# Threshold attention and an MLP mixer in one kernel: value groups two to a visit, one staging place for queries and keys, exponentials issued apart

## The chip, the cores and the metric

The kernel runs on one NeuronCore of a Trainium2 chip. The metric is the device time of one execution in microseconds (us). A profile is one execution recorded by the hardware profiler; its span runs from the first to the last instruction of the program. The engines are TensorE (PE in the profile, its weight loads PEld), VectorE (DVE), ScalarE (ACT), GpSimd (POOL) and SyncE (SP); DMAs are issued here from the queues of SP and ACT.

## What is computed

Eight batches, eight heads, 576 tokens, head size 64, all in float32. Attention keeps only scores that lie within tau of their row's maximum; its output, with the heads side by side (512 wide), goes through a token MLP and a channel MLP with residual sums.

```python
def _attn_ref(q, k, v, tau):
    scores = scale * np.matmul(q, k.transpose(0, 1, 3, 2))
    thresh = np.max(scores, axis=-1, keepdims=True) - tau
    scores = np.where(scores >= thresh, scores, -1000000000.0)
    scores = scores - np.max(scores, axis=-1, keepdims=True)
    attn = np.exp(scores)
    attn = attn / (np.sum(attn, axis=-1, keepdims=True) + 1e-09)
    return np.matmul(attn, v).astype(np.float32)

def _moe_ref(x, w_tok1, w_tok2, w_ch1, w_ch2):
    xt = x.transpose(0, 2, 1)
    h = np.maximum(xt @ w_tok1, 0.0) @ w_tok2
    u = x + h.transpose(0, 2, 1)
    h2 = np.maximum(u @ w_ch1, 0.0) @ w_ch2
    return (u + h2).astype(np.float32)
```

## The kernel before

**Units and visits.** Two heads make a pair, four pairs a batch (the code calls a batch a block, `b`). The work of two pairs is cut into nine units of 128 query rows: four of the first pair (t = 0 to 3), one that both pairs share for their last 64 rows (t = 4), four of the second (t = 5 to 8). The main loop (L529) visits the units in order, 144 of them in 16 windows of nine. The order of the instructions on every engine is the order in which this loop issues them; no scheduler changes it.

**One visit** of unit u issues, in this order:

- `scores(u)`: eight matmuls into two PSUM tiles (L301), a row maximum on VectorE for each head (L306), and a bias from it on GpSimd (L307).
- `norm(u - 1)`: reciprocals of the row sums on VectorE (L325, L326), a multiplication on GpSimd (L329).
- For unit u - 2 the transposition of its weights `e`. In block 0 TensorE does it (`turn`, L352), with copies on VectorE and ScalarE (L354). From block 1 on (`turn_blocks`) VectorE transposes 32 x 32 blocks into a tile T (L363), and when a group of two units is complete, 16 DMAs on SP's queue carry the blocks from T to their places in a tile eT (L373).
- `fill(0.4)`: mixer steps of an earlier block from a list, as many as a share of the visit's quota allows.
- `weigh(u)`: two Prelus (L316) read the scores out of PSUM into `e`, two Exps (L319) follow in place and give the row sums. All four are ScalarE's.
- `fill(0.6)`: more mixer steps.
- The loads for later pairs, the transposes of queries and keys of the next pair on VectorE (`prep`, L283) at t = 2 and t = 7, and last
- `values` (L385) for each group that is due: two matmuls of L403 and eight of L408 for a group of 256 query columns (each appears twice in the trace, since float32 goes through in two passes), and a copy from PSUM into xT on ScalarE (L413). A pair has two such groups, and a shared unit gives two of 64 columns. From block 1 on a group is due two visits after its DMAs were issued. That puts value groups into the visits with t = 1, 3, 5, 7 and (the two shared ones) 8.

**Mixer steps** are kept in the list `todo`: transposes of x (L425, copies L426 on ScalarE), the two matmuls of the token MLP (L434 with Relu L435 on ScalarE; L441 with an add L445 on VectorE), the first channel matmul (L463 with Relu L464 on ScalarE) and the second (L475, L479 with a copy L484 on VectorE and a store L485). The quota is the estimated cost of the list over the visits of a block. Until block 0 is through, there are none.

**Weights** come as 64-bit words in 31 pieces; `weight` turns them into float32 with small steps on ScalarE (L191, L193), VectorE (L201, L205, L209) and GpSimd (L215), and `load_piece` (L176) loads the next into one of four raw places from SP's queue. These steps run in the first 28 visits or so.

**Places.** PSUM: two tiles for scores (three in block 0), two `tr` tiles that transposes and value groups share, from block 1 on two `mm` tiles for the mixer. SBUF: staging tiles lq and lk for queries and keys in a pool with two places each; eT has two places, T two, `e` three.

**Loads of queries and keys.** A pair needs eight DMAs, four for each of lq and lk (L106). They are spread over visits t = 0 to 7, one part of lq and one of lk in each: on SP's queue in block 0 and on ScalarE's after. The loads for t = 0 to 3 belong to the pair whose `prep` is at t = 7, those of t = 4 to 7 to the one at t = 2 of the next window. Pair 1 is loaded at the start, before the values of pair 0 and the second weight piece (L242).

```python
        while due and due[0][0] <= u:
            _, b, p, c = due.popleft()
            values(b, p, c)
            if p == NP - 1 and c == 1:
                push(b)
```

Of the kernel before, what the change touches and what calls it, by code (L numbers as in the profile page):

```python
# [9 lines left out]
F32 = mybir.dt.float32  # L10
# [7 lines left out]
P = 128  # L18
# [3 lines left out]
def kernel(  # L22
# [26 lines left out]
    nc = tc.nc  # L49
    B, H, S, D = q.shape  # L50
# [14 lines left out]
    NK = 2 * S // P  # L65
# [4 lines left out]
    ld = ctx.enter_context(tc.tile_pool(name="ld", bufs=2))  # L70
    work = ctx.enter_context(tc.tile_pool(name="work", bufs=2))
# [11 lines left out]
    pairs = [(b, p) for b in range(B) for p in range(NP)]  # L83
# [9 lines left out]
    loaded = {}  # L93
    VL = 4
    vlast = [const.tile([P, P], F32, name=f"vl{i}") for i in range(VL)]

    def load_qk(n, eng, part=None):


        b, p = pairs[n]  # L100
        if n not in loaded:
            loaded[n] = [ld.tile([P, S // 32, 32], F32, tag=tag, name=f"{tag}_{n}") for tag in ("lq", "lk")]
        for i in range(4) if part is None else (part,):
            h, c = divmod(i, 2)
            for src, t, on in zip((q, k), loaded[n], eng):
                on.dma_start(  # L106
                    out=t[32 * i : 32 * i + 32], in_=src[b, 2 * p + h, :, 32 * c : 32 * c + 32].rearrange("(n t) d -> t n d", t=32)
                )

    def load_v(n):  # L110

        b, p = pairs[n]
        lv = ld.tile([P, NK, D], F32, tag="lv", bufs=4, name=f"lv_{n}")
        nc.sync.dma_start(out=lv, in_=v[b].rearrange("h s d -> (h s) d")[2 * S * p : 2 * S * p + 2 * S, :].rearrange("(c p) d -> p c d", p=P))
        vals[n] = lv
# [51 lines left out]
    def load_piece(i):  # L167
        if i >= len(pieces):
            return
        dst, src = pieces[i]  # L170
        rows = dst.shape[0]
        n = 1
        for d in dst.shape[1:]:
            n *= d
        raw = raw_at[i % NRAW][0:rows, 0 : n * (2 if wide(i) else 1)].bitcast(src.dtype)
        nc.sync.dma_start(out=like(raw, dst), in_=src)  # L176
        if wide(i):
            words = raw.bitcast(U32).rearrange("p (n w) -> p n w", w=2)
            h2 = work.tile([P, WMAX], F32, tag="o", name=f"h2_{i}")[0:rows, 0:n]
            raws[i] = like(words[:, :, 0], dst), like(words[:, :, 1], dst), like(h2, dst)  # L180
        else:
            raws[i] = like(raw, dst)
# [56 lines left out]
        weight(3 * i + 4 - steps_done)  # L239

    load_piece(0)
    load_qk(1, (nc.sync, nc.sync))  # L242
    load_v(0)
    for i in range(1, NRAW):
        load_piece(i)
# [24 lines left out]
    st = {}  # L270
    xTs = {}
    eTs = {}
    Ts = {}

    def in_blocks(b):
        return b > 0

    def prep(n):
        lq, lk = loaded.pop(n)
        made = []  # L280
        for src, name in ((lq, "qT"), (lk, "kT")):
            sb = work.tile([P, S], F32, tag=name, name=f"{name}_{n}")
            nc.vector.transpose(out=sb, in_=src.rearrange("p n d -> p (n d)"))  # L283
            made.append(sb)
        heads[n] = made
# [24 lines left out]
    def weigh(u):  # L310
        sc, bias = st.pop(u)
        rs = small.tile([P, 2], F32, tag="rs", name=f"rs_{u}")
        e = work.tile([P, 2 * S], F32, tag="e", bufs=3, name=f"e_{u}")
        for h in range(2):
            eh = e[:, S * h : S * h + S].rearrange("p (f x) -> p f x", f=2)
            nc.scalar.activation(out=eh, in_=sc[h][:, :, 0:HS], func=AF.Prelu, bias=bias[:, h : h + 1], scale=SCALE, alpha=STEEP)  # L316
        for h in range(2):
            eh = e[:, S * h : S * h + S]
            nc.scalar.activation(out=eh, in_=eh, func=AF.Exp, bias=ntau, accum_out=rs[:, h : h + 1])  # L319
        st[u] = e, rs  # L320

    def norm(u):
        e, rs = st[u]
# [8 lines left out]
    def group_of(u):  # L332

        b, p0, t = units[u]
        if t == SHARED:
            return (b, p0, "s"), 0, 1
        i, c = divmod(t - (t > SHARED), NI)
        return (b, p0 + i, c // 2), c % 2, 2

    def turn(u, third):  # L340

        key, place, n = group_of(u)
        e = st[u]
        if third == 0 and place == 0:
            eTs[key] = work.tile([P, NK * 2 * P], F32, tag="eT", name=f"eT_{u}")
        if third == 2:
            st.pop(u)
        eT = eTs[key][:, 0 : NK * n * P].rearrange("p (c x) -> p c x", c=NK)
        ps = ps_tr.tile([P, MAIN], F32, tag="tr", name=f"tr{third}_{u}")[:, 0 : 3 * P].rearrange("p (c x) -> p c x", c=3)
        for c in range(3):  # L350
            k0 = (3 * third + c) * P
            nc.tensor.transpose(out=ps[:, c, :], in_=e[:, k0 : k0 + P], identity=ident)  # L352
        on = nc.scalar.copy if third == 1 and u % 2 else nc.vector.tensor_copy
        on(out=eT[:, 3 * third : 3 * third + 3, P * place : P * place + P], in_=ps)  # L354

    def turn_blocks(u):

        key, place, n = group_of(u)
        e = st.pop(u)
        if place == 0:  # L360
            Ts[key] = work.tile([P, NK * 2 * P], F32, tag="T", name=f"T_{u}")
        T = Ts[key][:, 0 : NK * n * P]
        nc.vector.transpose(  # L363
            out=T.rearrange("p (a c n x) -> p c a n x", a=4, c=NK, n=n)[:, :, :, place, :],
            in_=e.rearrange("p (c a x) -> p c a x", c=NK, a=4),
        )
        if place == n - 1:
            del Ts[key]
            eTs[key] = work.tile([P, NK * 2 * P], F32, tag="eT", name=f"eT_{u}")
            w = NK * n * 32  # L370
            for a in range(4):
                for i in range(4):
                    nc.sync.dma_start(  # L373
                        out=eTs[key][32 * a : 32 * a + 32, w * i : w * i + w], in_=T[32 * i : 32 * i + 32, w * a : w * a + w]
                    )

    def split_middle(n):

        lv, vl = vals[n], vlast[n % VL]
        for h in range(2):  # L380
            r = slice(D * h, D * h + D)
            nc.gpsimd.tensor_copy(out=vl[r, r], in_=lv[r, NI, :])
        vals[n] = lv, vl
# [116 lines left out]
    def fill(share):  # L500
        nonlocal credit
        credit += share * quota
        while todo and credit > 0:
            cost, step = todo.popleft()
            credit -= cost
            step()
        if not todo:
            credit = 0.0
# [15 lines left out]

    prep(0)
    due = deque()
    b_now = 0
    LAG = 2
    for u in range(len(units) + LAG + 4):  # L529
        on = u < len(units)  # L530
        if u == UB:
            late.close()
            ps_mm = ctx.enter_context(tc.tile_pool(name="ps_mm", bufs=2, space=bass.MemoryType.PSUM))
        if on:
            b_now, p0, t = units[u]
            n = b_now * NP + p0
        w = u - LAG
        back = 0 <= w < len(units)
        if on:
            scores(u)  # L540
        if 0 < u <= len(units):
            norm(u - 1)
        if b_now:
            weight(2)
        if back:
            key, place, many = group_of(w)
            if in_blocks(key[0]):
                turn_blocks(w)
            else:
                for i in range(3):  # L550
                    turn(w, i)
            if place == many - 1:
                b, p, c = key
                if c == 0 and p % 2 == 0:
                    split_middle(b * NP + p)
                if c == "s":
                    split_middle(b * NP + p + 1)
                when = u + (2 if in_blocks(b) else 1)
                due += [(when, b, p + i, c) for i in range(2 if c == "s" else 1)]
        if b_now:  # L560
            fill(0.4)
        weight(2 if b_now else 1)
        if on:
            weigh(u)
        if b_now:
            fill(0.6)
        weight(2 if b_now else 1)
        if on:
            m = n + 2 + t // 4
            if t < 8 and m < len(pairs):  # L570
                load_qk(m, (nc.scalar if b_now else nc.sync,) * 2, t % 4)
                if t % 4 == 3:
                    load_v(m)
            if t == 2:
                prep(n + 1)
            if t == 7 and n + 2 < len(pairs):
                prep(n + 2)
# [5 lines that stand above are left out]
# [31 lines left out]
```

## Time and profile before

| | |
|---|---|
| times of five runs | 1395.74, 1398.53, 1400.26, 1400.70, 1401.69 us; median 1400.26 |
| profiled execution | 1400.26 us, its span 1398.5 us, mean granted TensorE clock 0.99 |
| busy: TensorE, VectorE, ScalarE, GpSimd | 1328.1, 587.6, 588.1, 357.5 us |
| costliest on TensorE | L479 389.1, L463 399.5, L301 190.2, L408 124.8, L441 77.0, L434 73.9 us |
| costliest on ScalarE | L319 220.1, L316 199.1, L464 85.9, L413 23.8 us |
| DMA | 128.34 MB, 92 GB/s on the mean |

A row of groups gives line, engine, operation, tiles and shape, then busy time and mean length; a row of the timeline gives start, length, engine, line, tiles and the number of instructions merged, and in brackets the idle time before the first of them with what ended it. A row of busy times by stretch gives for each of PE, PEld, DVE, ACT and POOL the busy time and the number of instructions, then the granted TensorE clock, the share of DMA engines that were busy, and GB/s. A busy TensorE is not one at its peak: at the change from one shape of matmul to another the next starts later, and the timeline counts that as busy; it shows only in the distance from start to start.

### The profile page before, as it was taken

What the parts mean: (1) busy time and instruction counts of PE and PEld (TensorE: products, weight loads), DVE (VectorE), ACT (ScalarE), POOL (GpSimd) and SP (SyncE); (2) the same over time, 40 slices, a digit from 0 to 9 for tenths busy, and PEclk for the clock granted to TensorE, in tenths of its full rate; (3) what the DMA queues carried; (4) which work ended last, traced back from release to release, by engine and by line L of the source; (5) the groups of instructions that cost most, each with busy time, mean ns of one, the idle gap of its engine ahead of it and who ended that gap; (6) DMA issues with size and microseconds to landing.
All of it is one profiled execution on the core that took longest, in us unless ns stands there. A gap on an engine that the chain in (4) does not pass through costs nothing.

```text
span 1398.5 us, 19515 instructions
## 1 busy us (share of the span) xinstructions
PE 1328.1 (95%) x6866; PEld 832.4 (60%) x6866; DVE 587.6 (42%) x1009; ACT 588.1 (42%) x1328; POOL 357.5 (26%) x683
## 2 busy tenths in 40 slices
PE   6776899999999999999999999999999999999998
PEld 3443465646565567565766567565657566576675
DVE  5789784454444444434243344433433454201000
ACT  5676564444454444443434435343434444220110
POOL 4466563232222222222222212221221222100000
PEclk9997999999999999999999999999999999999999
DMA  6354654444444434433434434443333433300000
GB/s 131 88 121 115 194 139 123 109 117 94 106 118 108 103 78 105 109 80 81 108 84 93 103 91 102 97 106 79 97 94 89 103 75 82 86 8 16 8 8 23
DMA packets 257376, 128.34 MB, mean 92 GB/s; under 512 B 208064, under 2 KB 221376, under 8 KB 257280
## 3 DMA queue, kind: packets, MB, share of 16 engines
q1 hardware_dynamic: 131632, 111.46, 30.4%
q10 hardware_dynamic: 125648, 15.64, 7.0%
q8 instruction: 55, 0.90, 0.3%
q14 instruction: 41, 0.34, 0.1%
HBM read 43.25 MB, written 9.44 MB: 38 GB/s over the span
## 4 chain that ended last, share of the span: by engine, by line
PE 86%; DVE 7%; ACT 2%; DMA 2%; SPq 1%; issue 1%; POOL 1%; ACTq 0%; DVEq 0%; POOLq 0%
PE c L479 27%; PE c L463 26%; PE sc L301 11%; PE pv L408 8%; PE t L434 5%; PE t L441 3%; DVE mx L306 3%; PE pv L403 3%; PE tx L425 1%; PE c L475 1%; PE pv_s L408 1%; DVE T L363 1%; SPq L373 1%; ACT e L316 1%; ACT e L319 1%
## 5 line engine op out<-in xcount | busy, mean ns | idle before, releaser
L306 DVE TENSOR_REDUCE mx<-sc 128x1 f32<-128x576 f32 x288 | 204.8, 752 | 528.2 <-PE sc L301 526.2
L463 PE MATMUL c<-xT,wc 128*128 128x256 f32 (+1 forms) x1920 | 399.5, 362 | 2.9 <-DVE xT L445 1.5
L479 PE MATMUL c<-wc,g 128*128 128x512 f32 x864 | 389.1, 596 | 0.0
L463 PEld LDWEIGHTS c<-xT,wc 128*128 128x128 f32 x1920 | 334.1, 190 | 73.4 <-issue 28.0
L307 POOL TENSOR_SCALAR bias<-mx,toff 128x1 f32<-128x1 f32 x288 | 79.6, 277 | 823.0 <-DVE mx L306 765.6
L316 ACT ACTIVATE e<-sc,bias 128x576 f32<-128x576 f32 x288 | 199.1, 739 | 155.0 <-POOL bias L307 154.7
L479 PEld LDWEIGHTS c<-wc,g 128*128 128x128 f32 x864 | 158.1, 190 | 175.1 <-issue 173.1
L464 ACT ACTIVATE g<-c 128x256 f32<-128x256 f32 (+1 forms) x240 | 85.9, 362 | 331.5 <-PE c L463 327.9
L329 POOL TENSOR_SCALAR e<-e,rr 128x576 f32<-128x576 f32 x288 | 218.8, 772 | 14.8 <-DVE rr L326 2.3
L319 ACT ACTIVATE e<-e,ntau 128x576 f32<-128x576 f32 x288 | 220.1, 772 | 0.0
L301 PE MATMUL sc<-kT,qT 64*128 64x288 f32 (+1 forms) x1280 | 190.2, 435 | 15.9 <-ACT e L316 8.6
L363 DVE STREAM_TRANSPOSE T<-e 128x1152 f32<-128x1152 f32 x126 | 172.5, 1369 | 16.2 <-DMA eT<-T 8.2
L301 PEld LDWEIGHTS sc<-kT,qT 64*128 64x128 f32 (+1 forms) x1280 | 103.8, 179 | 91.5 <-issue 45.0
L408 PE MATMUL pv<-eT,lv 128*64 128x256 f32 x1024 | 124.8, 387 | 0.0
L408 PEld LDWEIGHTS pv<-eT,lv 128*64 128x64 f32 x1024 | 75.9, 140 | 38.2 <-issue 2.6
L413 ACT COPY xT<-pv 128x256 f32<-128x256 f32 x64 | 23.8, 372 | 171.2 <-PE pv L408 167.2
L441 PE MATMUL t<-w,a 128*128 128x288 f32 x256 | 77.0, 429 | 16.5 <-DVE xT L445 9.9
L484 DVE COPY o<-c 128x512 f32<-128x512 f32 x36 | 24.5, 680 | 162.2 <-PE c L479 162.2
L434 PE MATMUL t<-x_sb,w 128*128 128x512 f32 x160 | 73.9, 610 | 0.7 <-ACT g L464 0.7
L441 PEld LDWEIGHTS t<-w,a 128*128 128x128 f32 x256 | 45.7, 193 | 43.8 <-DVE xT L445 18.0
L445 DVE TENSOR_TENSOR xT<-xT,t 128x288 f32<-128x288 f32 x64 | 28.0, 441 | 83.9 <-PE t L441 83.6
L319 ACT ACTIVATION_READ_ACCUMULATOR e<-e,ntau 128x1 f32 x288 | 56.9, 198 | 0.0
(48 smaller groups left out, 606.1 us busy)
## 6 DMA issues: line engine op xcount, KB each, us to landing
eT<-T SPq DMA_DIRECT2D x896, 72.0 KB, 2.0
scratch<-in_moe_w_ch_dram SPq DMA_DIRECT2D x24, 512.0 KB, 3.9
lv<-in_v_dram SPq DMA_DIRECT2D x32, 288.0 KB, 3.3
out_dram<-o SPq DMA_DIRECT2D x36, 256.0 KB, 2.2
eT<-T SPq DMA_DIRECT2D x224, 36.0 KB, 1.9
lk<-in_k_dram ACTq DMA_DIRECT2D x108, 72.0 KB, 2.7
lq<-in_q_dram ACTq DMA_DIRECT2D x104, 72.0 KB, 2.0
lq<-in_q_dram SPq DMA_DIRECT2D x24, 72.0 KB, 3.4
```

The lines of the kernel that those rows point to most:

```text
L301: nc.tensor.matmul(sc[h][rows, f, 0:HS], lhsT=qT[r, cols], rhs=kT[r, HS * f : HS * f + HS], start=True, stop=True)
L306: nc.vector.tensor_reduce(out=mx[:, c], in_=sc[h][:, :, 0:HS], axis=AX.XY, op=ALU.max)
L316: nc.scalar.activation(out=eh, in_=sc[h][:, :, 0:HS], func=AF.Prelu, bias=bias[:, h : h + 1], scale=SCALE, alpha=STEEP)
L319: nc.scalar.activation(out=eh, in_=eh, func=AF.Exp, bias=ntau, accum_out=rs[:, h : h + 1])
L329: nc.gpsimd.tensor_scalar(out=eh, in0=eh, scalar1=rr[:, h : h + 1], scalar2=1.0, op0=ALU.mult, op1=ALU.mult)
L363: nc.vector.transpose(out=T.rearrange("p (a c n x) -> p c a n x", a=4, c=NK, n=n)[:, :, :, place, :], in_=e.rearrange("p (c a x) -> p c a ...
L408: nc.tensor.matmul(to[r], lhsT=lv[:, j, :], rhs=eT[:, j], start=False, stop=(c == NI - 1), skip_group_check=True)
L434: nc.tensor.matmul(ps, lhsT=w1[:, t, P * m : P * m + P], rhs=x_sb[:, t, :], start=(t == 0), stop=(t == NT - 1))
L441: nc.tensor.matmul(ps, lhsT=s["a"][:, m, P * c : P * c + P], rhs=w2[:, m, HS * f : HS * f + HS], start=(m == 0), stop=(m == NTK - 1))
L463: nc.tensor.matmul(ps, lhsT=wc1[:, j, c, :], rhs=uT[:, c, GR * i : GR * i + n], start=(c == 0), stop=(c == NCC - 1))
L464: nc.scalar.activation(out=s["g"][:, j, 0:n], in_=ps, func=AF.Relu)
L479: nc.tensor.matmul(flat, lhsT=s["g"][:, j, P * t : P * t + P], rhs=wc2[:, j, :], start=False, stop=(j == NJ - 1), skip_group_check=True)
```

## The change

Four things are done together.

- From block 1 on, finished groups are held back: the first pair's two groups of values are due in one visit (t = 7), the two shared ones and the second pair's first group in another (t = 1 of the next window), the second pair's last one alone (t = 3). The shared unit gets an eT tile of its own, half the size and with one place (`eT1`); the large eT tiles keep two.
- lq and lk have one place each instead of two. So the loads of a pair are issued only after the transposes of the pair before: two DMAs in each of t = 3, 4, 5, 6 for the pair of t = 7, three at t = 8, three at t = 0 and two at t = 1 for that of t = 2. The loads of pair 1 move from the start to the first two visits.
- `weigh` issues a fifth of the visit's fill after the Prelus, a fifth after the first Exp and a fifth after the second; the `fill(0.6)` after it is left only for visits without a unit.
- `load_v` keeps its visits (t = 3 and 7).

```diff
--- before.py
+++ after.py
@@ -94,18 +94,19 @@
     VL = 4
     vlast = [const.tile([P, P], F32, name=f"vl{i}") for i in range(VL)]
 
-    def load_qk(n, eng, part=None):
+    def load_qk(n, eng, parts=range(8)):
 
 
         b, p = pairs[n]
         if n not in loaded:
-            loaded[n] = [ld.tile([P, S // 32, 32], F32, tag=tag, name=f"{tag}_{n}") for tag in ("lq", "lk")]
-        for i in range(4) if part is None else (part,):
+            loaded[n] = [ld.tile([P, S // 32, 32], F32, tag=tag, bufs=1, name=f"{tag}_{n}") for tag in ("lq", "lk")]
+        for part in parts:
+            i, which = divmod(part, 2)
             h, c = divmod(i, 2)
-            for src, t, on in zip((q, k), loaded[n], eng):
-                on.dma_start(
-                    out=t[32 * i : 32 * i + 32], in_=src[b, 2 * p + h, :, 32 * c : 32 * c + 32].rearrange("(n t) d -> t n d", t=32)
-                )
+            eng[which].dma_start(
+                out=loaded[n][which][32 * i : 32 * i + 32],
+                in_=(q, k)[which][b, 2 * p + h, :, 32 * c : 32 * c + 32].rearrange("(n t) d -> t n d", t=32),
+            )
 
     def load_v(n):
 
@@ -239,7 +240,6 @@
         weight(3 * i + 4 - steps_done)
 
     load_piece(0)
-    load_qk(1, (nc.sync, nc.sync))
     load_v(0)
     for i in range(1, NRAW):
         load_piece(i)
@@ -314,10 +314,15 @@
         for h in range(2):
             eh = e[:, S * h : S * h + S].rearrange("p (f x) -> p f x", f=2)
             nc.scalar.activation(out=eh, in_=sc[h][:, :, 0:HS], func=AF.Prelu, bias=bias[:, h : h + 1], scale=SCALE, alpha=STEEP)
+        st[u] = e, rs
+
+        if b_now:
+            fill(0.2)
         for h in range(2):
             eh = e[:, S * h : S * h + S]
             nc.scalar.activation(out=eh, in_=eh, func=AF.Exp, bias=ntau, accum_out=rs[:, h : h + 1])
-        st[u] = e, rs
+            if b_now:
+                fill(0.2)
 
     def norm(u):
         e, rs = st[u]
@@ -337,12 +342,16 @@
         i, c = divmod(t - (t > SHARED), NI)
         return (b, p0 + i, c // 2), c % 2, 2
 
+    def eT_tile(u, n):
+        tag, bufs = ("eT1", 1) if n == 1 else ("eT", 2)
+        return work.tile([P, NK * n * P], F32, tag=tag, bufs=bufs, name=f"{tag}_{u}")
+
     def turn(u, third):
 
         key, place, n = group_of(u)
         e = st[u]
         if third == 0 and place == 0:
-            eTs[key] = work.tile([P, NK * 2 * P], F32, tag="eT", name=f"eT_{u}")
+            eTs[key] = eT_tile(u, n)
         if third == 2:
             st.pop(u)
         eT = eTs[key][:, 0 : NK * n * P].rearrange("p (c x) -> p c x", c=NK)
@@ -366,7 +375,7 @@
         )
         if place == n - 1:
             del Ts[key]
-            eTs[key] = work.tile([P, NK * 2 * P], F32, tag="eT", name=f"eT_{u}")
+            eTs[key] = eT_tile(u, n)
             w = NK * n * 32
             for a in range(4):
                 for i in range(4):
@@ -524,6 +533,7 @@
 
     prep(0)
     due = deque()
+    held = []
     b_now = 0
     LAG = 2
     for u in range(len(units) + LAG + 4):
@@ -555,22 +565,35 @@
                     split_middle(b * NP + p)
                 if c == "s":
                     split_middle(b * NP + p + 1)
-                when = u + (2 if in_blocks(b) else 1)
-                due += [(when, b, p + i, c) for i in range(2 if c == "s" else 1)]
+                group = [(b, p + i, c) for i in range(2 if c == "s" else 1)]
+                if in_blocks(b):
+
+                    held += group
+                    if (p % 2, c) in ((0, 1), (1, 0), (1, 1)):
+                        due += [(u + 2,) + g for g in held]
+                        held.clear()
+                else:
+                    due += [(u + 1,) + g for g in group]
         if b_now:
             fill(0.4)
         weight(2 if b_now else 1)
         if on:
             weigh(u)
-        if b_now:
+        elif b_now:
             fill(0.6)
         weight(2 if b_now else 1)
         if on:
-            m = n + 2 + t // 4
-            if t < 8 and m < len(pairs):
-                load_qk(m, (nc.scalar if b_now else nc.sync,) * 2, t % 4)
-                if t % 4 == 3:
-                    load_v(m)
+
+
+            when = {3: (2, 0, 2), 4: (2, 2, 4), 5: (2, 4, 6), 6: (2, 6, 8), 8: (3, 0, 3), 0: (1, 3, 6), 1: (1, 6, 8)}
+            if u == 0:
+                load_qk(1, (nc.sync, nc.sync), range(0, 3))
+            if t in when:
+                m, lo, hi = when[t]
+                if n + m < len(pairs):
+                    load_qk(n + m, (nc.scalar if b_now else nc.sync,) * 2, range(lo, hi))
+            if t in (3, 7) and n + 2 + t // 4 < len(pairs):
+                load_v(n + 2 + t // 4)
             if t == 2:
                 prep(n + 1)
             if t == 7 and n + 2 < len(pairs):
```

## The prediction, made before the changed kernel was run

> **What bounds the kernel now.** I read the page first, then the busy times by stretch, then TensorE's timeline visit by visit (a visit is one turn of the loop over u; t is its place in a window of nine), then the waits. All sums are made against the profiled execution: 1400.26 us with a span of 1398.5 us, which is also the median of the runs shown.
>
> ```profile
> PE 1328.1 (95%) x6866; PEld 832.4 (60%) x6866; DVE 587.6 (42%) x1009; ACT 588.1 (42%) x1328; POOL 357.5 (26%) x683
> ...
> PE   6776899999999999999999999999999999999998
> ...
> DVE  5789784454444444434243344433433454201000
> ACT  5676564444454444443434435343434444220110
> ```
> ```profile
> 120.00:140.00 20.00, 12.72 (x44) 7.15 (x41) 19.16 (x26) 12.50 (x25) 13.52 (x15) 0.66 0.49 139
> 500.00:700.00 200.00, 198.53 (x1011) 124.69 (x1011) 77.07 (x131) 83.82 (x191) 46.33 (x100) 1.00 0.41 96
> 900.00:1100.00 200.00, 199.50 (x1013) 124.64 (x1012) 76.49 (x130) 82.06 (x186) 44.13 (x95) 1.00 0.39 91
> ```
>
> There are two regimes. Up to about 203 us (block 0 and the weights) TensorE idles a quarter of the time and VectorE is nearly full: 19.16 of 20 us at 120 to 140. After that TensorE is the bound at clock 1.00; its gaps over 0.1 us from 203 us to the end sum to only 15.9 us. So after 203 us only two things can move the end: TensorE time that is not arithmetic, and these gaps. The issue orders of the two programs show that every visit has the same matmuls of the fill (mixer) steps in both; on TensorE only the value groups change visit.
>
> **Part 1: value groups together.** Before, values stand in five visits of a window (t = 1, 3, 5, 7, 8); after, in three: at t=7 two groups, at t=1 the two shared ones and then (pair 1, group 0), at t=3 one. What does a neighbour save? The kernel before has one such case, the two shared groups (columns: start, time, engine, line):
>
> ```profile
> 324.43 0.34 PE L403 MATMUL pv_s<-eT,vl 128*64 128x64 f32 x4
> 324.60 0.64 PE L408 MATMUL pv_s<-eT,lv 128*64 128x64 f32 x16
> 325.07 0.29 PE L403 MATMUL pv_s<-eT,vl 128*64 128x64 f32 x4
> 325.18 0.64 PE L408 MATMUL pv_s<-eT,lv 128*64 128x64 f32 x16
> 325.75 1.24 PE L301 MATMUL sc<-kT,qT 64*128 64x288 f32 x8
> ```
>
> From start to start the first L403 four take 0.17 us, the second 0.11; the first L408 sixteen take 0.47, the second, which runs into the scores, 0.57. A group that follows a group therefore saves 0.06 at its entry and 0.10 at the exit of the one ahead: 0.16 us. A fill that runs into scores ends as late as one that runs into values (24 matmuls of L463 take 5.38 us either way), so nothing is given back there. Two joints a window, 14 windows, of which the first lies where VectorE bounds: 26 x 0.16 = **4.2 us less**. Bounds: 0, if the entry is paid again while eight landing waits are processed, and 28 x 0.3 = 8.4, if 256-column groups save twice as much.
>
> **Part 2: the third group of t=1 (a new wait).** It takes the PSUM place of the first shared group, so it waits for that group's copy (L413) on ScalarE. Queued behind it on TensorE are the next visit's scores. Clean case above: the first group ends at 325.24, its copy ran 325.28 to 325.49, the second group ends at 325.75: no wait. But in the new order ScalarE has, ahead of the copies, the last Exp, perhaps a Relu eviction, and two load issues (0.34 and 0.58 us). I went through the 14 visits with the fill times of before. In five the fills are L479 steps, which VectorE evicts; the last Exp ends 4.2 us after the scores and the fills at 4.9 us or later: no wait. In seven a Relu is the last: it is ready 0.1 us after the fills, issues done at 1.0, copy done at 1.25, wanted at 1.2: 0.1 each at most. In two (before: scores at 196.90 and 1052.08) the last Exp stands behind the last Relu: Exp ends 5.9 after the scores where the group is wanted at 4.9, plus copy: 1.3; and 0.45. Together **2.3 us more**; bounds 0 and 14 x 1.3 = 18.
>
> The Trainium skill (TensorEngine Tiling (Array Packing), PSUM Bottleneck) warns that packing speeds up TensorE but not the emptying of PSUM, which may become the bound. It speaks against this part; by it all 14 visits would wait, by the rows above two do.
>
> **Part 3: the exponentials taken apart.** Fill steps now issue after the Prelus, after the first Exp and after the second, so a Relu no longer stands behind both Exps. This pays only where TensorE waits for one:
>
> ```profile
> 804.24 0.76 ACT L319 ACTIVATE e<-e,ntau 128x576 f32<-128x576 f32 x1
> ...
> 805.00 0.42 ACT L464 ACTIVATE g<-c 128x128 f32<-128x128 f32 x2
> 805.31 1.24 PE L441 MATMUL t<-w,a 128*128 128x288 f32 x4 [2.33 <-ACT g L464]
> ```
>
> In the new order the first of these Relus follows the Prelus, which end at 803.58, and the second follows the first Exp. So L441 starts at about 803.9 (1.4 earlier), the next L463 waits 0.15 for the second Relu. 1.25 us, and the same pattern at 1130.86: 2.5. A like wait of 0.44 at 478.83 goes: 0.4. A third kind goes by Part 1, the values at t=5 of this window, which waited for x_sb copies behind the Exps:
>
> ```profile
> 440.54 0.60 PE L425 MATMUL tx<-ident,xT 128*128 128x128 f32 x4
> 442.21 0.65 PE L403 MATMUL pv<-eT,vl 128*64 128x256 f32 x4 [1.07 <-issue]
> ```
>
> 1.1. The waits for VectorE's adds (1.26 at 321.33, 1.60 at 330.73 and others, 6.5 together) stay: VectorE's order is the same. **4.0 us less**; bounds 0 and 8.3 + 1.1 = 9.4, all waits of TensorE for Relus and copies. The price: the last Exp can end up to 1.5 us after the fills, but its first reader on VectorE (L325) comes after the next visit's two maxima, 2.7 us after the fills: covered.
>
> **Part 4: loads into one place.** At the start eight q/k loads leave the front of SP's queue:
>
> ```profile
> 10.26 1.86 SPq L176 DMA_DIRECT2D scratch<-in_moe_w_tok_dram  x3
> 15.79 0.67 ACT L191 ACTIVATE scratch<-scratch 128x512 int32<-128x512 uint32 x1 [2.03 <-DMA scratch<-in_moe_w_tok_dram]
> 17.69 2.29 PE L301 MATMUL sc<-kT,qT 64*128 64x288 f32 x4 [3.10 <-ACT e L316]
> ```
>
> The three weight pieces then issue some 5 us earlier, ScalarE loses its 2.03 us wait, and the scores at 17.69 come 1.7 us earlier (the next limit is the bias, at 15.6). Against it, the last loads of a pair now issue one visit ahead of the transposes (L283) instead of four. In block 0 I place them after the weight load of the same visit: landings at 22.3, 50.4, 73.3, 99.3 us against transposes at 24.3, 52.4, 72.4, 99.0: two short waits of VectorE, 0.9 and 0.3. Later a load lands some 3.7 us after the fills of its visit, while the transposes come at 4.5 or more: hidden. That the place is free is no new wait: the transposes that free it come before the maxima that ScalarE has already waited for. Net **0.5 us less**; bounds 1.7 less and, if each of the 28 later transposes waited 1 us and VectorE had no slack, 28 more; VectorE is 42% busy, so I stay near the low end.
>
> The Trainium skill (DMA: Bandwidth & Descriptors, Rules for kernel authors) says to issue a DMA early and wait late; this part does the opposite. By the rule, 28 landings of 2.7 us would be exposed, 76 us; by the rows they keep a visit's work in front of them.
>
> **Part 5: shorter visits at t=5.** The transpose T (L363) at t=7 writes the place that the block DMAs of t=5 read, and comes 2.3 us earlier. The 16 DMAs land 11.5 to 13 us after their T; I count waits of up to 2.9 us on VectorE (window at 240), behind them the q/k transposes and the next maxima. The two value groups of that visit (4.6 us) cover them; an output copy (L484) at 783.93 does not quite: **0.5 us more**, bounds 0 and 14 x 1 = 14. The values of t=7 keep 0.6 us or more to the landing.
>
> Sum: -4.2 + 2.3 - 4.0 - 0.5 + 0.5 = -5.9; 1400.3 - 5.9 = **1394.4 us**.
>
> **Rivals.**
> *ScalarE becomes the bound of t=1 (slower).* The copies stand behind Relu, Exp, two issues in a row; 1.3 us in each of 14 visits is 18 instead of 2.3: 1400.3 - 8.7 + 0.5 + 18 = 1410. For it: two visits do so by my count. Against: the sequencer issues loads while ScalarE still works (at 789.69, beside L435 at 789.68). It eats the gain from 0.6 us a visit and makes the kernel slower by 0.3% from 0.9.
> *The change does not do what it says (same).* Entries are paid again and evictions only swap places; 1.5 us are left: 1399.
> *More goes than counted (faster).* Most of the 15.9 us of gaps move away with the new rhythm and the start gains 1.7: 1388.
>
> **How the numbers follow.** Forecast 0.52 (1391 to 1396), same 0.24 (1396 to 1402), ScalarE rival 0.14 (1402 to 1412), more 0.10 (1386 to 1391). A difference of 0.3%, 4.2 us, is about what a measurement of this kernel can tell from no change, so under 1396.1 counts as faster: 0.52 + 0.10 = 0.62; within 0.25; slower 0.13. The range leaves out the outer halves of the first and last case: 1389 to 1403.
>
> **What would show it.** Right: pairs of L403/L408 runs at t=7 with about 0.11 us between, no scores between them; the 2.33 us waits at half or less; the 203 us mark up to 2 us earlier. Wrong: TensorE waiting for L413's copies in more than a few visits, VectorE waiting for q/k landings after 203 us, or TensorE gaps after 203 us above 16 us.

## The result, and the profile after

The changed kernel takes 1400.27 us (median of 29 runs, 1396.44 to 1404.0), the kernel before on the same chip 1401.11 us; the ratio is 0.9995 with a 95% interval of 0.9989 to 1.0002. So the change makes no difference that can be measured; a gain of 5.9 us had been forecast. The profiled execution took 1398.5 us with a span of 1396.7 us and a mean granted clock of 0.99. In the changed kernel the lines of `values` are L412, L417 and L422 (before: L403, L408, L413), the mixer's L434 to L493 are the former L425 to L484, the Exps stand in L323, T in L372, its DMAs in L382.

The page and the stretches that were shown of before:

```profile
PE 1325.1 (95%) x6866; PEld 834.1 (60%) x6866; DVE 587.8 (42%) x1009; ACT 590.4 (42%) x1328; POOL 357.3 (26%) x683
...
PE   6777789999999999999999999999999999999998
...
DVE  5788865453444444434343444433443454101000
ACT  5776654544445444443433534453434444120110
```
```profile
120.00:140.00 20.00, 16.32 (x79) 8.70 (x77) 17.93 (x26) 13.25 (x26) 13.30 (x14) 0.81 0.42 128
500.00:700.00 200.00, 198.76 (x1010) 125.51 (x1008) 79.54 (x135) 83.98 (x191) 46.30 (x100) 1.00 0.40 96
900.00:1100.00 200.00, 199.48 (x1003) 124.80 (x1002) 78.37 (x133) 83.84 (x188) 46.32 (x100) 1.00 0.38 92
```

The page hides nearly everything: the same two regimes, the same busy shares. Only the slice at 175 to 210 us (the sixth digit of PE, 8 where before had 9) and a sum over TensorE's gaps tell more: from 203 us on, the gaps over 0.1 us sum to 17.8 us, where before had 15.9 and fewer were forecast.

**The joints work.** Two groups at t=7, in TensorE's timeline after (answering to the pair of shared groups shown of before):

```profile
458.60 0.65 PE L412 MATMUL pv<-eT,vl 128*64 128x256 f32 x4
459.08 1.90 PE L417 MATMUL pv<-eT,lv 128*64 128x256 f32 x16
460.81 0.60 PE L412 MATMUL pv<-eT,vl 128*64 128x256 f32 x4
461.24 1.90 PE L417 MATMUL pv<-eT,lv 128*64 128x256 f32 x16
463.06 1.24 PE L301 MATMUL sc<-kT,qT 64*128 64x288 f32 x8
```

From 458.60 to the scores at 463.06 are 4.46 us; a group alone takes 2.30 (before, 201.72 to 204.03: 2.31). So 0.14 us are saved. The three groups of t=1 take 3.47 us where nothing waits (in six of the twelve windows after the first two), against 1.31 + 2.30 apart: 0.14 again.

**The third group of t=1 does not.** TensorE's and ScalarE's timeline after at the first such visit, and SP's queue beside them:

```profile
200.83 6.29 SPq L382 DMA_DIRECT2D eT<-T  x10
201.09 0.32 ACTq L106 DMA_DIRECT2D lq<-in_q_dram  x1
202.23 0.36 ACTq L106 DMA_DIRECT2D lk<-in_k_dram  x1
202.91 0.33 ACT L422 COPY xT<-pv_s 128x64 f32<-128x64 f32 x2 [2.36 <-DMA eT<-T]
...
203.17 1.12 PE L412 MATMUL pv<-eT,vl 128*64 128x256 f32 x4 [3.53 <-ACT xT L422]
...
204.08 2.89 PE L417 MATMUL pv<-eT,lv 128*64 128x256 f32 x16
```

The last Exp was done at 200.55. ScalarE then has two load issues ahead of the copies L422. These issues began at 201.09 and 202.23, though one takes 0.32 us; where nothing holds them two follow at 0.36 us, as in the kernel before:

```profile
807.53 0.32 ACTq L106 DMA_DIRECT2D lq<-in_q_dram  x1
807.89 0.51 ACTq L106 DMA_DIRECT2D lk<-in_k_dram  x1
```

The trace puts the wait of 2.36 us down to a landing of SP's eT<-T, and its semaphores show how. The DMAs of both queues tell of their landings on the same eight counters, and an issue waits until the earlier DMA on its counter has landed. The one at 201.09 waited for an eT<-T that SP had issued at 199.01 and that landed at 201.07, the one at 202.23 for one issued at 200.20 that landed at 202.21. From 195 us on, 25 of the changed kernel's 195 load issues on ScalarE began within 0.06 us of such a landing, against 2 of 192 before.

TensorE, which needs the PSUM place, stood for 3.53 us, and then ran slower: 2.89 us for what takes 1.90. The granted clock by stretches of 4 us says why (column after the five engines; in the trace's clock record it is 0.5 from 202.68 to 206.09 us):

```profile
200.00:204.00 4.00, 0.83 (x4) 0.53 (x6) 0.00 (x0) 0.88 (x4) 0.00 (x0) 0.83 0.64 146
204.00:208.00 4.00, 4.00 (x26) 2.15 (x22) 0.00 (x0) 0.37 (x1) 0.00 (x0) 0.74 0.50 130
```

The visit of unit 28 lasted from 193.44 to 206.90 us, 13.46 us; before, with one group, 7.13. Its three groups take 8.64 us instead of 3.47. In seven later windows the three groups take 0.2 to 0.6 us more than 3.47 (2.3 us in all). Here is one with its copy late, t=1 of the next window:

```profile
271.07 0.34 PE L412 MATMUL pv_s<-eT,vl 128*64 128x64 f32 x4
...
271.82 0.64 PE L417 MATMUL pv_s<-eT,lv 128*64 128x64 f32 x16
272.71 0.65 PE L412 MATMUL pv<-eT,vl 128*64 128x256 f32 x4 [0.25 <-ACT xT L422]
273.19 1.90 PE L417 MATMUL pv<-eT,lv 128*64 128x256 f32 x16
275.02 1.24 PE L301 MATMUL sc<-kT,qT 64*128 64x288 f32 x8
```

**The split of the exponentials works, but a new wait follows it.** The place shown of before, in the whole timeline after:

```profile
802.96 0.27 ACT L473 ACTIVATE g<-c 128x128 f32<-128x128 f32 x1
803.12 0.78 ACT L323 ACTIVATE e<-e,ntau 128x576 f32<-128x576 f32 x1
...
803.28 1.24 PE L450 MATMUL t<-w,a 128*128 128x288 f32 x4 [0.82 <-ACT g L473]
...
803.88 0.27 ACT L473 ACTIVATE g<-c 128x128 f32<-128x128 f32 x1
```

The Relus now stand after the Prelus and between the Exps (L323), and TensorE's wait is 0.82 us instead of 2.33. But the next token step, two steps on, waits longer than before (0.37 us for ScalarE):

```profile
809.98 1.24 PE L450 MATMUL t<-w,a 128*128 128x288 f32 x4 [1.34 <-DVE xT L454]
```

The wait of 1.07 us at 442.21 is gone; its visit now has no values:

```profile
441.26 2.74 PE L488 MATMUL c<-wc,g 128*128 128x512 f32 x6
443.84 0.60 PE L434 MATMUL tx<-ident,xT 128*128 128x128 f32 x4
444.37 1.24 PE L301 MATMUL sc<-kT,qT 64*128 64x288 f32 x8
```

**The start.** The weight pieces issue at 4.83 instead of 10.26 us, ScalarE's wait of 2.03 us for them is gone, and the scores that came at 17.69 come at 16.99:

```profile
4.83 1.85 SPq L177 DMA_DIRECT2D scratch<-in_moe_w_tok_dram  x3
...
15.11 0.66 ACT L192 ACTIVATE scratch<-scratch 128x512 int32<-128x512 uint32 x1
16.99 2.29 PE L301 MATMUL sc<-kT,qT 64*128 64x288 f32 x4 [0.95 <-ACT e L316]
```

### The profile page after: what moved, and what is told of

Read it like the earlier page. It is cut to its first block, busy times and chain, and to the rows that moved or that the text cites. A ratio compares the mean times of both kernels' runs of the same rounds, so it can differ in the third digit from the quotient of the medians.

```text
span 1396.7 us, 19563 instructions
## 1 busy us (share of the span) xinstructions
PE 1325.1 (95%) x6866; PEld 834.1 (60%) x6866; DVE 587.8 (42%) x1009; ACT 590.4 (42%) x1328; POOL 357.3 (26%) x683
## 4 chain that ended last, share of the span: by engine, by line
PE 86%; DVE 7%; DMA 2%; ACT 1%; POOL 1%; issue 1%; SPq 1%; ACTq 0%; DVEq 0%; POOLq 0%
PE c L488 27%; PE c L472 26%; PE sc L301 11%; PE pv L417 8%; PE t L443 5%; PE t L450 3%; DVE mx L306 3%; PE pv L412 2%; PE tx L434 1%; DVE T L372 1%; PE c L484 1%; SPq L382 1%; DMA eT<-T 1%; PE pv_s L417 1%; DMA scratch<-in_moe_w_ch_dram 1%
## 5 line engine op out<-in xcount | busy, mean ns | idle before, releaser
L323 ACT ACTIVATE e<-e,ntau 128x576 f32<-128x576 f32 x288 | 220.5, 770 | 0.0
L372 DVE STREAM_TRANSPOSE T<-e 128x1152 f32<-128x1152 f32 x126 | 172.5, 1369 | 25.1 <-DMA eT<-T 19.5
L417 PE MATMUL pv<-eT,lv 128*64 128x256 f32 x1024 | 126.9, 392 | 0.0
L417 PEld LDWEIGHTS pv<-eT,lv 128*64 128x64 f32 x1024 | 76.7, 142 | 39.5 <-issue 3.7
L493 DVE COPY o<-c 128x512 f32<-128x512 f32 x36 | 24.5, 680 | 158.2 <-PE c L488 158.2
L422 ACT COPY xT<-pv 128x256 f32<-128x256 f32 x64 | 23.7, 371 | 132.2 <-PE pv L417 126.3
L323 ACT ACTIVATION_READ_ACCUMULATOR e<-e,ntau 128x1 f32 x288 | 56.4, 196 | 0.0
```

The source lines that it names most:

```text
L372: nc.vector.transpose(out=T.rearrange("p (a c n x) -> p c a n x", a=4, c=NK, n=n)[:, :, :, place, :], in_=e.rearrange("p (c a x) -> p c a ...
L417: nc.tensor.matmul(to[r], lhsT=lv[:, j, :], rhs=eT[:, j], start=False, stop=(c == NI - 1), skip_group_check=True)
```

## The experiments

Two theories after the first look. *A:* the gains are there, and t=1 eats them, where the copies for the third group stand on ScalarE behind load issues. *B:* they are eaten elsewhere, by the one staging place and by VectorE's waits for landings. Differences in us are ratio times 1401 us, with 95% intervals in brackets; they are all against the kernel before on the same chip, and two runs are compared by these differences.

**1. Loads behind the values.** Changed kernel, the `while due` loop put ahead of the loads:

```diff
         weight(2 if b_now else 1)
+        while due and due[0][0] <= u:
+            ...
+                push(b)
         if on:
             when = {...}
```

> The changed kernel with one thing moved: the q/k loads, lv loads and q/k transposes of a visit are issued after its value groups instead of before, so on ScalarE's queue no load stands between the last Exp or Relu and the copies L422. Theory A (the gain of the joined groups is eaten at t=1, where the copies wait behind load issues that themselves wait for a landing of SP's DMAs): the TensorE waits for L422, 3.5 us at 203 and 2.3 us in seven later visits, go except for about 0.4 us where an Exp is late, and with the 3.5 us gap the half-speed group after it (1.3 us): 6 to 7 us faster than the changed kernel, 1394, 0.4 to 0.5% faster than before. Theory B (the gain is eaten elsewhere, by the single staging place or by VectorE's longer waits for landings at T): less than 1.5 us of difference, 1399 to 1401.

Measured: 1393.23 us, ratio 0.9937 (0.9922 to 0.9952), 8.8 us below before (6.7 to 10.9): A's number and somewhat more. The loads of v and the q/k transposes of the visit moved with the loop too, but they stand on other queues than the copies. At unit 28 the third group waits 0.58 us instead of 3.53 and the groups run at full speed; later the three groups take 3.47 us in every window but one (3.71).

**2. No joined groups.** Changed kernel, every group due two visits after its DMAs again:

```diff
-                if in_blocks(b):
-                    held += group
-                    ...
-                else:
-                    due += [(u + 1,) + g for g in group]
+                due += [(u + (2 if in_blocks(b) else 1),) + g for g in group]
```

> The changed kernel without the holding back: every group of values is due two visits after its DMAs as before; single staging place and split Exps stay. Theory A: the joints' 3.6 us are lost, and so are the waits at t=1 (7 us with the slow group), so it is as fast as or up to 4 us faster than the changed kernel: 1396 to 1400. Theory B (staging place or split Exps cost the time): slower than the changed kernel by the joints' 3.6 us, 1403 to 1404.

Measured: 1396.35 us, ratio 0.9962 (0.9949 to 0.9975), 5.3 below before (3.5 to 7.1). The joining, as the changed kernel does it, costs 4.6 us, though each joint saves 0.14. That is near A's range (up to 4 us); B's number was missed.

**3. Exponentials together again.** Changed kernel, `weigh` and its fill as before:

```diff
-        st[u] = e, rs
-        if b_now:
-            fill(0.2)
         for h in range(2):
             ...
-            if b_now:
-                fill(0.2)
+        st[u] = e, rs
 ...
-        elif b_now:
+        if b_now:
             fill(0.6)
```

> The changed kernel with both Exps issued together again and fill(0.6) after them. Theory A: the wait of 2.3 us behind both Exps comes back twice (0.8 now), and at t=1 the last Exp is never behind a Relu that waits for the fills, but the loads still are in front of the copies: the waits for L422 stay within 1 us of what they are, 1 to 2 us slower than the changed kernel, 1401 to 1402. Rival (the split Exps delay the copies, not the loads): the waits for L422 fall below 2 us in all and it is 2 to 4 us faster, 1396 to 1398.

Measured: 1409.11 us, ratio 1.0043 (1.0026 to 1.0059), 6.0 above before (3.6 to 8.3). Both forecasts were wrong: taking the split away costs 6.7 us, neither 1 to 2 nor a gain. The trace shows 2.33 us of waiting at 809.77 and 1136.25 again, but also new waits of 0.55 us behind VectorE at 820.12 and 1148.21, and copies that come 0.9 us late at 347.84 and 417.15. The wait at 1136.25 is followed by 3.41 us at half clock (last section).

**4. Other groups joined.** Changed kernel, none is third at t=1; the two shared ones stay at t=8 as before and pair 1's two stand together at t=3:

```diff
-                    if (p % 2, c) in ((0, 1), (1, 0), (1, 1)):
+                    if (p % 2, c) in ((0, 1), (0, "s"), (1, 1)):
```

> The changed kernel with the groups joined otherwise: the two of the first pair at t=7, the two shared ones at t=8, the two of the second pair at t=3 of the next window. As many joints (28), but no visit has three groups, so no group needs a PSUM place that is still to be copied in the same visit. Price: the block DMAs of the next window's first group wait on SP's queue for the values at t=3. Theory A: the waits for L422 vanish, joints stay: 6 to 7 us faster than the changed kernel, 1393 to 1394; the DMAs come about 9 us late but are due four visits later. Theory B: within 1.5 us of the changed kernel.

Measured: 1393.54 us, ratio 0.9937 (0.9922 to 0.9953), 8.8 below before (6.6 to 10.9). A again: as many joints, none of which waits for a copy. Against run 2, which differs in the joints alone, that is 3.5 us less: the joints' worth.

**5. The start alone.** Kernel before, pair 1's loads put behind the weight pieces:

```diff
     load_piece(0)
-    load_qk(1, (nc.sync, nc.sync))
     load_v(0)
     for i in range(1, NRAW):
         load_piece(i)
     load_v(1)
+    load_qk(1, (nc.sync, nc.sync))
```

> The kernel before with one edit: the queries and keys of pair 1 are issued behind the pieces of the MLP weights at the start, not ahead of them. It measures the start term alone. In the changed kernel the first maxima of unit 20 came at 120.40 us, 1.9 us earlier than before. If the place of these loads is the reason, 1.5 to 2 us below before. If that gain belongs to the six later loads that the changed kernel puts off as well, or is the spread of the clock in the first 200 us, within 0.7 us of before.

Measured: 1401.47 us, ratio 1.0003 (0.9993 to 1.0013). Nothing that can be measured. The first maxima of unit 20 differ from before's by -1.9 us in the changed kernel, by -0.8, +0.5, +2.6 and -0.5 in runs 1 to 4, which have the same start: one trace does not show a start gain of 1.7 us.

**6. The split alone.** Kernel before, with the changed kernel's `weigh` and fill (the reverse of edit 3).

> The kernel before with one edit: the two exponentials of a visit taken apart by fill steps (part 3 alone). By the waits of TensorE in the changed kernel's trace (0.5 us less at each of the two places near 805 and 1130 us, 1.1 us at 442.21, 0.5 us between 478 and 503 us) 2 to 3 us below before. If the split by itself is worth what its removal cost the changed kernel, 6 to 9 us below before; then the changed kernel loses that much elsewhere.

Measured: 1395.46 us, ratio 0.9955 (0.9939 to 0.997), 6.3 below before (4.2 to 8.5), the second case of what was expected. From unit 36 to unit 139 its trace is 5.9 us shorter, and TensorE's gaps show where: 1.5 us each at the two places near 805 and 1130, 1.07 at 442, 1.1 between 478 and 503. The last 0.8 us are in no gap: they lie in the distances between matmuls. And the next token step waits 0.37 us as it did before, not 1.34.

**7. The new places of the loads alone.** Kernel before, with `load_qk`, the table of visits and `bufs=1` of the changed kernel; groups, e tiles and Exps as before.

```diff
-            loaded[n] = [ld.tile([P, S // 32, 32], F32, tag=tag, name=f"{tag}_{n}") for tag in ("lq", "lk")]
+            loaded[n] = [ld.tile([P, S // 32, 32], F32, tag=tag, bufs=1, name=f"{tag}_{n}") for tag in ("lq", "lk")]
 ...
+            when = {3: (2, 0, 2), 4: (2, 2, 4), 5: (2, 4, 6), 6: (2, 6, 8), 8: (3, 0, 3), 0: (1, 3, 6), 1: (1, 6, 8)}
```

> The kernel before with the new places of the loads alone: one staging place, the new table of visits, pair 1's loads put off (part 4 alone); groups of values, e tiles and exponentials as before. Theory A (the loss is the joined groups' copies behind load issues at t=1): without joined groups the loads cost nothing, 1 to 2 us below before, the start's gain. Theory B (the one place and its later landings cost the time by themselves): 2 to 4 us above before.

Measured: 1406.25 us, ratio 1.0035 (1.0023 to 1.0047), 4.9 above before (3.2 to 6.6). B's direction, and more than its 2 to 4 us: part 4 alone costs, without any joined group. But not by B's reason. TensorE's timeline of this run, at the place near 811 us of before:

```profile
808.83 1.24 PE L441 MATMUL t<-w,a 128*128 128x288 f32 x4
809.91 1.05 PE L463 MATMUL c<-xT,wc 128*128 128x128 f32 x8
812.30 1.24 PE L441 MATMUL t<-w,a 128*128 128x288 f32 x4 [1.34 <-DVE xT L445]
...
815.95 1.16 PE L463 MATMUL c<-xT,wc 128*128 128x128 f32 x8 [0.55 <-DVE xT L445]
```

and of the kernel before:

```profile
808.54 1.24 PE L441 MATMUL t<-w,a 128*128 128x288 f32 x4
809.61 1.05 PE L463 MATMUL c<-xT,wc 128*128 128x128 f32 x8
811.03 1.24 PE L441 MATMUL t<-w,a 128*128 128x288 f32 x4 [0.37 <-ACT g L464]
```

The same steps in the same order, VectorE and ScalarE alike to 0.01 us, and yet the step at 812.30 waits until VectorE has done the add L445 of the token step before it, which on VectorE stands behind two maxima and a transpose T of 1.36 us. In the trace this matmul (`tok2(1, 0)` of block 4, and the same of block 6) waits for VectorE's counter, where before's waits for ScalarE's. So with the loads elsewhere the step must have been handed the other of the two `mm` tiles, the one that VectorE empties. That is theory C.

The sum fits: from unit 36 to unit 139 this trace is 4.5 us longer than before's, and 3.9 us of it are TensorE's gaps over 0.1 us. Those behind the add L445 grew from 6.5 to 11.2 us, those behind the Relu L464 fell from 8.0 to 7.3.

**8. The loads of t=0 and t=1 on SyncE's queue.** Changed kernel:

```diff
-                    load_qk(n + m, (nc.scalar if b_now else nc.sync,) * 2, range(lo, hi))
+                    load_qk(n + m, (nc.scalar if b_now and t > 1 else nc.sync,) * 2, range(lo, hi))
```

> The changed kernel with one edit: the loads of the visits t=0 and t=1 are issued on SyncE's queue, not on ScalarE's; visits, groups and order otherwise the same. Theory A (ScalarE stands in those two visits in load issues that wait for landings, and the copies for the third group stand behind them): the copies come in time, 5 to 7 us below before, like the kernel whose loads stand behind the values. Theory B (landings come late with one staging place, whoever issues): as the changed kernel, within 1 us of before; above it if SyncE's transposing transfers are put off by these loads.

Measured: 1391.33 us, ratio 0.9924 (0.991 to 0.9939), 10.6 below before (8.5 to 12.6), more than A's 5 to 7. At unit 28 the third group waits 0.58 us for its copy instead of 3.53:

```profile
197.93 0.33 ACT L422 COPY xT<-pv_s 128x64 f32<-128x64 f32 x2
...
198.21 0.65 PE L412 MATMUL pv<-eT,vl 128*64 128x256 f32 x4 [0.58 <-ACT xT L422]
198.69 1.90 PE L417 MATMUL pv<-eT,lv 128*64 128x256 f32 x16
```

The step of theory C waits for ScalarE again in this program, and its wait is 0.37 us at 800.04 and 1123.67; run 1, where it was 1.34, is 1.8 us slower (the intervals of the two overlap). VectorE waits 22.9 us for q loads in this run, 1.8 in the changed kernel, and the kernel is still one of the two fastest: those waits must be hidden for the most part.

**9. Theory C on the kernel before.** Run 7 with the loads of t=0 and t=1 on SyncE's queue (the edit of run 8).

> The kernel before with the new places of the loads alone (as in the run of part 4 alone), but the loads of the visits t=0 and t=1 on SyncE's queue. Theory C (the new places make two fill steps of blocks 4 and 6 take a PSUM buffer that VectorE's addition must free, where before's take one that ScalarE frees: 1.34 us instead of 0.37 us, and 0.55 us a step later, in two places): in the built program of this kernel those steps wait for ScalarE again, so 3 to 4 us of the 4.9 us that part 4 alone cost are gone, 0 to 2 us above before. If the one staging place or the later landings cost the time by themselves, it stays, 4 to 6 us above before.

Measured: 1401.72 us, ratio 1.0003 (0.9991 to 1.0014), 0.4 above before (-1.3 to 2.0). The cost of part 4 is gone, with the staging place still single. The edit also takes issues off ScalarE, so this run alone doesn't tell C from issues that hold ScalarE up; but in run 7 TensorE's waits behind ScalarE had not grown. TensorE's timeline at the step:

```profile
809.20 1.05 PE L463 MATMUL c<-xT,wc 128*128 128x128 f32 x8
810.62 1.24 PE L441 MATMUL t<-w,a 128*128 128x288 f32 x4 [0.36 <-ACT g L464]
```

All fourteen traces agree: at this step of block 4 the wait is 1.34 us, for VectorE, in the changed kernel and in runs 1, 2, 3, 4, 7 and 11, which issue the loads of t=0 and t=1 on ScalarE in the new visits; in the kernel before and in runs 5, 6, 8, 9, 10 and 12 it is 0.36 or 0.37 us, for ScalarE.

**10. Run 8 without the split.** The edits of runs 3 and 8 together.

> The changed kernel with the exponentials together again and the loads of t=0 and t=1 on SyncE's queue. If split exponentials are worth the same with joined groups as alone (6.3 us), 4 to 5 us below before (10.5 less 6.3). If the groups need the split (the copies of a third group stand behind both exponentials), 0 to 2 us below before or above it.

Measured: 1395.79 us, ratio 0.9955 (0.994 to 0.9971), 6.3 below before (4.1 to 8.4), more than either case expected. The split is worth 4.3 us here, less than its 6.3 alone, but the intervals overlap.

**11. Runs 1 and 4 together.**

> The changed kernel with the groups joined so that none is third at t=1, and the loads behind the values as well. Theory A (the loads hurt only where copies for a third group stand behind them): the second edit adds nothing to the first, 8 to 9.5 us below before, as with the other groups alone. If the load issues hold ScalarE up at other places too, 10 us or more below before.

Measured: 1393.57 us, ratio 0.9942 (0.9924 to 0.9961), 8.1 below before (5.5 to 10.6). The second edit adds nothing that these intervals show, as A has it: held issues hurt where a third group waits.

**12. Runs 4 and 8 together.**

> The changed kernel with the groups joined so that none is third at t=1, and the loads of t=0 and t=1 on SyncE's queue. By the two edits' own traces: the loads on SyncE's queue gave 10.5 us, of which 2 us by the fill steps' buffers of blocks 4 and 6 (theory C), and the other groups' joints saved some 1.6 us more than the changed kernel's; so 11 to 13 us below before. If the other groups bring nothing beside the moved loads, 10 to 11 us below before.

Measured: 1389.96 us, ratio 0.9915 (0.9898 to 0.9933), 11.9 below before (9.4 to 14.3): the best time of all, though not told apart from run 8; whether the other joints add anything here stays open.

## Why the prediction was wrong

The mechanisms named were nearly all there. The sum failed, mostly in one step: part 2 came out 5.8 us larger than forecast.

- **Part 1 (4.2 us less): held.** 0.14 instead of 0.16 us a joint, 3.6 us for 26; run 4 against run 2 gives 3.5.
- **Part 2 (2.3 us more): the step that failed.** Run 1 against the changed kernel gives 8.1 us, run 4 the same; in the changed kernel's trace 7.4 us can be pointed at: 5.17 at unit 28 (8.64 against 3.47), where 1.3 was forecast, and 2.25 in seven later visits. The prediction had this queue right, Exp, Relu, two issues, copy, and reckoned the issues at their own length, 0.34 and 0.58 us, from a row where nothing held them. They are held until SP's transfer on the same counter has landed, and everything behind them on ScalarE is held with them. That wait was in no row that the prediction had priced. It also reckoned a wait of TensorE at its length; after the one of 3.53 us the third group took 3.73 us instead of 2.30, 1.4 us more at half clock.
- **Part 3 (4.0 us less): right in kind, too small.** Alone 6.3 us, of which 5.9 stand in the trace. The two great waits give 1.5 each instead of 1.25. Between 478 and 503 us 1.1 goes instead of 0.4: the waits there for VectorE's adds, which the prediction left as they were, fall from 2.7 to 1.7 us. Another 0.8 us comes from closer matmuls, which it did not count. The wait at 442.21 was put down to the joined groups; in run 6, which has none, it is gone as well, so it belonged to the Exps.
- **Part 4 (0.5 us less): wrong in sign.** Alone it costs 4.9 us, and with the split 1.0 (run 2 against run 6) to 1.8 us (run 1 against run 8), both within their intervals; the traces of runs 2 and 6 differ by 3.0 from unit 36 to unit 139. The reason was none of those weighed (start, landings, transposes): mixer steps, two of them above all, wait for VectorE instead of ScalarE. The prediction compared the order of the steps in the two programs, which is the same, and not what each waits for, which is not. Of the start's 1.7 us, 0.7 stand at the scores of 17.69, and none can be seen in run 5 or at unit 20.
- **Part 5 (0.5 us more): nothing.** VectorE's waits for T did grow, from 8.2 to 19.5 us, no run takes them apart, and none shows a cost. (The landings follow their T by up to 15.2 us in before's trace until 1200 us, not by 13 at most.)

```profile
DVE T L372 <- DMA eT<-T: 19.5, 41, 2.7
```

Measured terms: -3.6 + 8.1 - 6.3 + 1.5 = -0.3 us (+1.2 with 3.0 for part 4), and the change measured -0.7 (-1.5 to 0.3). One of the prediction's own signs of being wrong came true: TensorE's gaps after 203 us are above 16 us. Of the rivals, "ScalarE becomes the bound of t=1" had the right place and mechanism; it was taken as all or nothing in 14 windows (18 us), and came as 5.2 us in one visit and 0.2 to 0.6 in seven others. "The change does not do what it says" had the right time for a wrong reason: each part does what it says.

What stays open: why the place of the loads decides which `mm` tile a step is handed. That the tile differs is read from whose counter the step waits for; the traces don't show how it is chosen.

## What to carry to other kernels

Before work that another engine waits for is put behind a DMA issue on a compute engine's queue, price that issue at its wait and not at its length; if the issue isn't urgent, put it behind the urgent work or on a queue that nobody waits for (here 8 to 10 us for moving five load issues of each window). When a change moves anything that shares pools or counters with the rest, compare the waits of the two programs and not only the order. And join work so that the follower does not need what the leader has just filled: run 4 had as many joints as the change, and no wait for a copy.

## What the runs showed of the chip that was not expected

- **A stall can cost more than its length, depending on where it falls.** In every trace here the granted clock changes only at whole multiples of 3.41 us from its first change. From 195 to 1385 us it fell to 0.5 for one such stretch wherever TensorE had been idle for 2.21 us or more of the stretch before: 3.03 us in the changed kernel, and 2.21 to 2.33 in runs 3, 5, 9 and 10, each time in one of the two 2.33 us waits that part 3 is about. The split takes these waits away; half speed for 3.41 us is, by estimate, 1.7 us more. It did not fall where the idle time was 2.00 us or less. So run 3's stall of 2.93 us, 2.00 of it in one stretch and 0.93 in the next, cost only its length, while its wait of 2.33 us at 1136.25 fell into one stretch (the granted clock in the two stretches behind them stands ahead of the last two columns):

```profile
206.69 0.65 PE L407 MATMUL pv<-eT,vl 128*64 128x256 f32 x4 [2.93 <-ACT xT L417]
207.17 1.90 PE L412 MATMUL pv<-eT,lv 128*64 128x256 f32 x16
...
1136.25 2.04 PE L445 MATMUL t<-w,a 128*128 128x288 f32 x4 [2.33 <-ACT g L468]
```
```profile
208.20:211.50 3.30, 3.30 (x23) 1.86 (x19) 1.23 (x2) 0.46 (x2) 0.27 (x1) 1.00 0.46 113
1136.60:1139.90 3.30, 3.30 (x12) 2.63 (x10) 0.45 (x1) 0.00 (x0) 0.00 (x0) 0.50 0.46 115
```

The Trainium skill (TensorE: Matmul & The Clock Gate, What's actually happening) tells of a free-running window of 3413 ns, as seen here, and gives at least one idle window, about 3.4 us, as what halves the clock; here 2.21 us of idleness within one were enough.

- **Load issues held on ScalarE** stood 1.14 us apart at unit 28 in place of 0.36, until transfers of SP's queue had landed. The same loads on SyncE's queue, among the transposing transfers, went with 22.9 us of VectorE's waiting for q loads in run 8, and the time still fell.
